# Attention and two MoE layers on one core: a second staging buffer for the weight chunks, gate constants pinned, fills sent later, and another split of the first dense unit's roundings

## The chip, the cores and the metric

One core of one Trainium2 chip runs the whole program in one launch. The metric is the device time of that launch in microseconds (us). Engines by the names of the profile: PE is TensorE, DVE is VectorE, ACT is ScalarE, POOL is GpSimd, SP is SyncE, which issues most DMAs.

## What is computed

The reference chains three parts, the output of one being the input of the next:

```
def phi(x):
    proj = np.einsum('bhsd,df->bhsf', x, w_phi)
    proj = proj - np.max(np.abs(proj), axis=-1, keepdims=True)
    return np.concatenate([np.exp(proj), np.exp(-proj)], axis=-1)
q_p, k_p = (phi(q), phi(k))
kv = np.einsum('bhsf,bhsd->bhfd', k_p, v)
z = np.sum(k_p, axis=2)
num = np.einsum('bhsf,bhfd->bhsd', q_p, kv)
den = np.einsum('bhsf,bhf->bhs', q_p, z)[..., None] + 1e-06
attn = num / den                      # 8 batches, 8 heads, 576 x 64
...
h = x @ w_in                          # 4608 x 512 @ 512 x 2048
g = h * np.cos(h)
x = g @ w_out                         # dense layer
...
logits = x @ w_gate + modality_bias[modality_id]
e_idx = np.argmax(logits, axis=1)     # top 1 of 8 experts
h = np.maximum(x[mask] @ w1[e], 0.0)
out[mask] = gate_w[mask, None] * (h @ w2[e])
```

`w_in` and `w_out` of the dense layer arrive as float64, two 32-bit words a number; the kernel has to make float32 parts of them itself.

## The kernel before

**Attention (L47 to L278).** The 64 (batch, head) pairs are taken in 16 items of two batches and two heads. An item has five turns; a turn handles up to two chunks of 128 tokens of both heads. In a turn PE transposes q and k (L121), ACT copies them out of PSUM (L124), PE projects them (L136), DVE takes the maximum of the absolute values (L141; the `m_q` reduction is a turn's first DVE instruction) and subtracts it (L142), ACT makes the exponentials of k (L153, L154), PE transposes the q side (L189), ACT makes the exponentials of q (L195, tiles `qx`, 5 buffers), PE sums the products of k and v (L174) and, for the item before, the quotient's parts (L210); DVE divides (L215 to L217), PE turns the result (L226), ACT copies it (L228) and an item's result leaves by one DMA (L231). The order of these is written out as a generator; each `next(att)` is one half turn, ten of them an item. Instructions inside `keep(...)` stay in program order on their engine; the others are placed by the tile framework's scheduler, within what buffers allow.

**Decode of the dense weights (L387 to L442).** The two dense weights are cut into 32 chunks of 512 KB, in the order of `seq`. `stage()` sends the DMA of the next chunk (L395 for `w_in`, L397 for `w_out`) into a staging tile `st`; `decoding()` makes two float32 parts of it: ACT takes abs of the high words (L431, or L418 in the form without steps), DVE does four passes of 128x512 (L432 to L435, or L419 to L423) of which the last two read the chunk again, ACT rounds to the high part (L436 or L424), `stage()` is called for the next chunk, and POOL makes the low part (L428; DVE L427 in the paced form). Fourteen chunks are decoded in steps during items 1 to 11 of attention (`work`, four calls an item), all pinned; the call that ends one chunk also makes the abs and the first pass of the next, so three calls make a chunk; six more, not pinned, during the last 20 half turns (`head`); twelve more, the paced ones, are decoded in three parts a round inside the first dense unit. For the first 14 chunks the staging tile is the one buffer `sx`; later chunks go to `raw_k` and `raw_q`. So a chunk's DMA is sent when the chunk before it has been read for the last time.

**Dense layer.** Nine units of 512 tokens, each with 16 slices of 128 columns. A round is 12 matmuls of 128x512 into `ph` (L472) for one slice, 12 matmuls into four accumulators (L506) for the slice three back, and `act()` (L481 to L498): ACT rounds ph/(2 pi) to integers `n` (L485), DVE subtracts (L487), ACT sine and square (L489, L490), DVE `g` (L492), DVE rounds `g` to its high part `gh` (L494), POOL takes the rest `gl` (L495). `split_x` makes the two parts of the next unit's x: DVE rounds (L462), POOL or, for the fourth, DVE subtracts (L463).

**Constants.** `consts()` (L973) writes four fills to DRAM, `tab` (L978) and rows of `x1d` (L981, L984), then runs `gate_consts` (L281), which loads the gate's weight and the modality ids (`mi`, L292, L293) and prepares small tiles on DVE. It is started at half turn 9 of attention and goes on at 17 to 25.

The rest (the gate, the routing, the experts) the change doesn't touch.

```
for n in range(170-TAIL):
    next(att)
    if n==8: stage()
    if n==9: next(setup)
    ...
    if 10<=n and n%10 in (0,2,4,6): next(work,None)
```

Of the kernel before, what the change touches and what calls it, by code (L numbers as in the profile page):

```python
# [11 lines left out]
F32 = mybir.dt.float32  # L12
# [18 lines left out]

SHARED = {"raw_k":(1024,2),"raw_q":(1024,2),"ke":(1024,4),"qe":(1024,3),"xT":(1152,4),"xw":(1024,6),"kt":(512,3),"qt":(512,3),"kvh":(512,4),"kvl":(512,4),"kvt":(512,2),"wx":(1024,5),"sx":(1024,1)}

def shared_tiles(tc, ctx):
    sp=ctx.enter_context(tc.tile_pool(name="shared",bufs=1))
# [6 lines left out]
def attention(tc, ctx, S, ps, ident, q, k, v, w_phi, xt):  # L44
# [138 lines left out]
    def qexp(i,g):  # L183

        n=GR[g][1]; tt=ts.pop(("q",i,g))
        pt=ps.tile([P,512],F32,tag="tr",name=f"ptt_{i}_{g}")
        for c in range(n):
            for s in range(2):
                keep(nc.tensor.transpose(pt[:,(2*c+s)*P:(2*c+s+1)*P],tt[:,(s*n+c)*F:(s*n+c+1)*F],ident))  # L189
        w=n*P  # L190
        x=qx[i,g]=ap.tile([P,1024],F32,tag="qx",name=f"qx_{i}_{g}",bufs=5)[:,:4*w].rearrange("p (h k c) -> p h k c",h=2,k=2)
        def vec():
            pv=pt[:,:2*w].rearrange("p (h c) -> p h c",h=2)
            for kk,sign in ((0,1.0),(1,-1.0)):
                nc.scalar.activation(x[:,:,kk,:],pv,AF.Exp,scale=sign)  # L195
        return vec
# [86 lines left out]
def gate_consts(tc, ctx, cpool, ps, ident, modality_id, modality_bias, w_gate, wgt, tp):  # L283
# [35 lines left out]
    nc.sync.dma_start(wgt[:,:],gt)  # L319
    yield  # L320

    nc.vector.memset(f32(g2[:,:,8:16]),0.0)
    fold=cpool.tile([16,8],F32,name="fold")
    V("tensor_tensor",fold,ident[0:16,0:8],ident[0:16,8:16],ALU.add)
    tri=cpool.tile([P,P],BF16,name="tri"); V("tensor_copy",tri,tf)
    one=cpool.tile([P,P],BF16,name="one"); nc.vector.memset(one,1.0)
    rev=cpool.tile([P,8],F32,name="rev"); V("tensor_copy",rev,ri)
    run=cpool.tile([P,8],F32,name="run0"); V("tensor_copy",run,rg)
    base=cpool.tile([P,8],F32,name="base"); V("tensor_copy",base,rg)
# [1 line left out]

    num=cpool.tile([P,8],F32,name="num"); V("tensor_copy",num,nm)
    slot=cpool.tile([1,25],F32,name="slot"); V("tensor_copy",slot,sl)
    ones=cpool.tile([1,16],F32,name="ones"); nc.vector.memset(ones,1.0)
    mf=tp.tile([P,36],F32,name="mf"); V("tensor_copy",mf,mi[:,:,:,0].rearrange("p a c -> p (a c)"))
    mz=tp.tile([P,36],F32,name="mz"); V("tensor_scalar",mz,mf,-1.0,1.0,op0=ALU.mult,op1=ALU.add)
    yield
# [8 lines left out]
def moes(tc, ctx, consts, S, ps, ident, att, end_att, xt, w_in, w_out, x1d, tab, wgt, w1, w2, out):  # L346
# [13 lines left out]
        return S({"fr":"kt","n":"qt","gh":"kvh","gl":"kvl"}[tag],name,dt)  # L360
    def pair(tag,name):

        if tag=="wl": t=late[0].tile([P,1024],F32R,tag="wl",name=name,bufs=12)
        else: t=S(tag,name,F32R)
        return t[:,0:512],t[:,512:1024]
    pj=[]
# [36 lines left out]
    def decoding(paced=False,steps=False):  # L403

        x=next(todo,None)
        if x is None: return
        decoded[0]+=1
        f,which=x
        v=st[f,which].rearrange("p (f w) -> p f w",w=2)
        H=v[:,:,1]; L=v[:,:,0]  # L410
        t=xtile("gl" if decoded[0]<=19 else "row",f"d_t{which}_{f}",F32)
        ti=t.bitcast(I32)
        h,l=pair(wtag[which][f],f"w{which}_{f}")
        (win,wout)[which][f]=(h,l)
        keep=tc.keep_in_program_order if paced else lambda ins: ins
        def one():

            nc.scalar.activation(t,H.bitcast(F32),AF.Abs,scale=2.0**-112)  # L418
            keep(nc.vector.tensor_scalar(t,t,F32_MAX,None,op0=ALU.min))  # L419
            keep(nc.vector.tensor_scalar(ti,ti,3,None,op0=ALU.logical_shift_left))  # L420
        def two():
            keep(nc.vector.scalar_tensor_tensor(ti,L,29,ti,op0=ALU.logical_shift_right,op1=ALU.bitwise_or))
            keep(nc.vector.scalar_tensor_tensor(ti,H,-0x80000000,ti,op0=ALU.bitwise_and,op1=ALU.bitwise_or))  # L423
            nc.scalar.copy(h,t)  # L424
            stage()
        def three():
            if paced: keep(nc.vector.tensor_tensor(l,t,f32(h),ALU.subtract))  # L427
            else: nc.gpsimd.tensor_tensor(l,t,f32(h),ALU.subtract)  # L428
        if steps:
            keep=tc.keep_in_program_order  # L430
            keep(nc.scalar.activation(t,H.bitcast(F32),AF.Abs,scale=2.0**-112))  # L431
            yield keep(nc.vector.tensor_scalar(t,t,F32_MAX,None,op0=ALU.min))  # L432
            yield keep(nc.vector.tensor_scalar(ti,ti,3,None,op0=ALU.logical_shift_left))
            yield keep(nc.vector.scalar_tensor_tensor(ti,L,29,ti,op0=ALU.logical_shift_right,op1=ALU.bitwise_or))
            keep(nc.vector.scalar_tensor_tensor(ti,H,-0x80000000,ti,op0=ALU.bitwise_and,op1=ALU.bitwise_or))  # L435
            keep(nc.scalar.copy(h,t)); stage(); three()  # L436
        elif paced: parts.append([one,two,three])
        else:
            one(); two(); three()
# [41 lines left out]
    def act(u,f):  # L481

        ph=phs.pop((u,f))
        n=xtile("n",f"n_{u}_{f}",I32)
        nc.scalar.activation(n,ph,AF.Copy,scale=INV2PI)  # L485
        g=xtile("fr",f"fr_{u}_{f}",F32)
        nc.vector.scalar_tensor_tensor(g,ph,INV2PI,n,op0=ALU.mult,op1=ALU.subtract)  # L487
        decode_part(2); decode_part(0)
        nc.scalar.activation(g,g,AF.Sin,scale=math.pi)  # L489
        nc.scalar.activation(g,g,AF.Square)  # L490
        score(1)
        nc.vector.scalar_tensor_tensor(g,g,-0.5,ph,op0=ALU.add,op1=ALU.mult)  # L492
# [451 lines left out]
def kernel(  # L944
# [27 lines left out]

    def consts():  # L973
        with tc.tile_pool(name="fill", bufs=1) as tp:
            pre = tp.tile([P, 8 * REG // P, 2], I32, name="pre")
            nc.gpsimd.memset(pre[:, :, 0], NTOK)
            nc.gpsimd.memset(pre[:, :, 1], 0)
# [48 lines left out]
```

## Time and profile before

| | before |
|---|---|
| median of 3 runs | 1726.19 us (1724.95 to 1727.88) |
| profiled execution, its own time | 1725.87 us |
| span of the profiled execution | 1723.9 us |
| PE busy | 1635.5 us (95%) |
| DVE busy | 1148.1 us (67%) |
| ACT busy | 828.2 us (48%) |
| POOL busy | 428.6 us (25%) |
| granted PE clock, mean | 0.976 of full speed |

How to read it: busy time is the sum of an engine's instructions, the span is from the first to the last of them. In the rows further down, `A <- B` behind a line says what that instruction waited for last, and the number ahead of it how long the engine stood idle. PEclk is the clock granted to PE as a share of full speed. A row of a window has its start and end and its length in us, then the busy us of PE, of PE's weight loads, DVE, ACT and POOL (each with the count of instructions), PEclk, the busy share of the DMA engines, and GB/s.

### The profile page before, as it was taken

What the parts mean: (1) busy time and instruction counts of PE and PEld (TensorE: products, weight loads), DVE (VectorE), ACT (ScalarE), POOL (GpSimd) and SP (SyncE); (2) the same over time, 40 slices, a digit from 0 to 9 for tenths busy, and PEclk for the clock granted to TensorE, in tenths of its full rate; (3) what the DMA queues carried; (4) which work ended last, traced back from release to release, by engine and by line L of the source; (5) the groups of instructions that cost most, each with busy time, mean ns of one, the idle gap of its engine ahead of it and who ended that gap; (6) DMA issues with size and microseconds to landing.
All of it is one profiled execution on the core that took longest, in us unless ns stands there. A gap on an engine that the chain in (4) does not pass through costs nothing.

```text
span 1723.9 us, 33528 instructions
## 1 busy us (share of the span) xinstructions
PE 1635.5 (95%) x13076; PEld 1397.7 (81%) x13076; DVE 1148.1 (67%) x2331; ACT 828.2 (48%) x1529; POOL 428.6 (25%) x353
## 2 busy tenths in 40 slices
PE   7898889989989999999999999999799999999997
PEld 5788878988768888888888888888678998899986
DVE  4677768786866767777776767664556655655635
ACT  4556657665433333334343434343335655655645
POOL 0000000003232333333333333342221221111212
PEclk8899989999989999999999999999899999999999
DMA  6434444433221010101010101000368675766656
GB/s 192 116 117 136 116 121 136 141 110 100 75 75 36 7 44 7 38 13 38 13 38 13 38 13 37 7 2 24 122 199 316 223 241 195 253 220 217 224 177 223
DMA packets 142544, 190.06 MB, mean 110 GB/s; under 512 B 64535, under 2 KB 89239, under 8 KB 142370
## 3 DMA queue, kind: packets, MB, share of 16 engines
q1 hardware_dynamic: 134578, 166.74, 30.7%
q0 software_dynamic: 7792, 21.02, 3.7%
q8 instruction: 108, 1.77, 0.4%
q14 instruction: 66, 0.54, 0.1%
HBM read 157.98 MB, written 30.51 MB: 109 GB/s over the span
## 4 chain that ended last, share of the span: by engine, by line
PE 72%; DVE 12%; DMA 8%; ACT 3%; issue 3%; SPq 1%; POOL 1%; DVEq 0%; POOLq 0%; ACTq 0%
PE ph L472 19%; PE acc L506 14%; PE mh L756 11%; PE po L768 10%; PE acc L511 4%; PE pj L136 3%; DMA st<-in_moe_w_in_dram 3%; PE pn L210 3%; PE kv L174 2%; DMA tab<-rec,pi 1%; DMA st<-in_moe_w_out_dram 1%; DVE x L462 1%; PE pt L121 1%; DMA raw<-in_moe_w_dram 1%; DVE d_t L423 1%
## 5 line engine op out<-in xcount | busy, mean ns | idle before, releaser
L472 PE MATMUL ph<-x,w 128*128 128x512 f32 x1728 | 425.7, 394 | 10.9 <-DVE x L462 5.9
L472 PEld LDWEIGHTS ph<-x,w 128*128 128x128 f32 x1728 | 322.8, 188 | 87.7 <-DVE x L462 9.6
L495 POOL TENSOR_TENSOR gl<-fr,gh 128x512 fp32r<-128x512 f32 x144 | 216.9, 1509 | 443.6 <-DVE gh L494 390.2
L716 DVE TENSOR_TENSOR m<-raw,m 128x512 fp32r<-128x512 f32 x320 | 210.2, 695 | 142.3 <-ACT m L715 142.3
L506 PE MATMUL acc<-w,gh 128*128 128x512 f32 x896 | 276.8, 390 | 0.0
L715 ACT CAST m<-raw 128x512 fp32r<-128x512 f32 x320 | 187.2, 618 | 69.3 <-PE mh L756 33.4
L756 PEld LDWEIGHTS mh<-xT,m 128*128 128x128 f32 x1728 | 212.3, 194 | 7.1 <-DVE hl L759 2.2
L756 PE MATMUL mh<-xT,m 128*128 128x256 f32 x1728 | 213.4, 285 | 4.6 <-DVE hl L759 2.0
L485 ACT ACTIVATE n<-ph 128x512 int32<-128x512 f32 x144 | 85.8, 596 | 269.1 <-PE ph L472 268.9
L506 PEld LDWEIGHTS acc<-w,gh 128*128 128x128 f32 x896 | 169.0, 189 | 35.1
L487 DVE SCALAR_TENSOR_TENSOR fr<-ph,n 128x512 f32<-128x512 f32 x144 | 99.2, 689 | 133.2 <-ACT n L485 117.7
L768 PE MATMUL po<-m,hh 128*128 128x512 f32 x576 | 181.3, 396 | 2.0 <-ACT hh L758 2.0
L536 DVE SCALAR_TENSOR_TENSOR junk<-x1T,wg 128x512 f32<-128x512 f32 x224 | 180.9, 808 | 0.0
L506 PE MATMUL acc<-w,gl 128*128 128x512 f32 x448 | 174.8, 390 | 0.0
L489 ACT ACTIVATE fr<-fr 128x512 f32<-128x512 f32 x144 | 91.1, 633 | 153.6 <-DVE fr L487 153.0
L492 DVE SCALAR_TENSOR_TENSOR fr<-fr,ph 128x512 f32<-128x512 f32 x144 | 98.7, 685 | 77.2 <-ACT fr L490 77.2
L768 PEld LDWEIGHTS po<-m,hh 128*128 128x128 f32 x576 | 106.0, 190 | 22.4 <-ACT hh L758 2.4
L806 POOL DMA_INDIRECT out_dram<-o,mrec x39 | 41.6, 1068 | 289.6 <-ACT o L805 281.0
L768 PE MATMUL po<-m,hl 128*128 128x512 f32 x288 | 113.1, 393 | 0.1
L210 PE MATMUL pn<-kvz,qx 128*64 128x65 f32 x2304 | 90.2, 233 | 18.7 <-DVE xs L217 16.5
L210 PEld LDWEIGHTS pn<-kvz,qx 128*64 128x64 f32 x2304 | 79.5, 145 | 29.5 <-issue 16.5
L506 PEld LDWEIGHTS acc<-w,gl 128*128 128x128 f32 x448 | 84.4, 188 | 17.7
(197 smaller groups left out, 2366.9 us busy)
## 6 DMA issues: line engine op xcount, KB each, us to landing
raw<-in_moe_w_dram SPq DMA_DIRECT2D x171, 512.0 KB
xt<-xo SPq DMA_DIRECT2D x16, 576.0 KB
xr<-xt SPq DMA_DIRECT2D x36, 256.0 KB
raw_k<-in_k_dram SPq DMA_DIRECT2D x32, 256.0 KB
raw_q<-in_q_dram SPq DMA_DIRECT2D x32, 256.0 KB
v<-in_v_dram SPq DMA_DIRECT2D x64, 128.0 KB
st<-in_moe_w_in_dram SPq DMA_DIRECT2D x16, 512.0 KB
st<-in_moe_w_out_dram SPq DMA_DIRECT2D x16, 512.0 KB
```

Source lines behind the costliest of these rows:

```text
L210: keep(nc.tensor.matmul(o[64*c:64*c+64],x[:,h,sg,t*P+64*c:t*P+64*c+64],kvs[i,bb][:,2*h+sg,:],start=sg==0,stop=sg==1,skip_group_check=True))
L472: nc.tensor.matmul(ph,A[:,ws],xhl[u,d][k],start=n[0]==0,stop=n[0]==11); n[0]+=1
L487: nc.vector.scalar_tensor_tensor(g,ph,INV2PI,n,op0=ALU.mult,op1=ALU.subtract)
L489: nc.scalar.activation(g,g,AF.Sin,scale=math.pi)
L492: nc.vector.scalar_tensor_tensor(g,g,-0.5,ph,op0=ALU.add,op1=ALU.mult)
L495: nc.gpsimd.tensor_tensor(gl,g,f32(gh),ALU.subtract)
L506: nc.tensor.matmul(accs[u][c],A[:,ws],B,start=(f==0 and k==0),stop=(f==NF-1 and k==2))
L536: return lambda: tc.keep_in_program_order(nc.vector.scalar_tensor_tensor(junk,x1T[u,c],1.0,wg[e],op0=ALU.mult,op1=ALU.mult,accum_out=lgs[u ...
L715: keep(nc.scalar.copy(h,a))
L716: keep(nc.vector.tensor_tensor(l,a,f32(h),ALU.subtract))
L756: nc.tensor.matmul(ph[:,f2*T:(f2+1)*T],A[:,ws],B[d//2][:,xs],start=n==0,stop=n==11); n+=1
L768: nc.tensor.matmul(po[c],A[:,ws],B,start=(f==0 and j==0),stop=(f==NF2-1 and j==2))
```

## The change

It gives `sx` two buffers and the tile of the q exponentials four in place of five. The first chunk is staged at half turn 4 and the second at 14, where before the first was staged at 8 and the others each at the end of the decode ahead of it; with the calls of `stage()` inside the decode left as they are, a chunk is from then on staged one decode earlier. The table of staging tiles follows (16 chunks in `sx`, then `raw_k`, `raw_q`), one more chunk is decoded ahead of the first dense unit (21, with a new place in `head`), and the pool `wl` has 11 buffers for 12. The three memsets of the gate constants are pinned. The four fills are written behind the gate constants, at half turn 25. In `act()`, in the rounds that carry a paced decode, ACT makes `gh` and DVE makes `gl`.

```
-...,"sx":(1024,1)}
+...,"sx":(1024,2)}
...
-        x=qx[i,g]=ap.tile([P,1024],F32,tag="qx",name=f"qx_{i}_{g}",bufs=5)[...]
+        x=qx[i,g]=ap.tile([P,1024],F32,tag="qx",name=f"qx_{i}_{g}",bufs=4)[...]
...
-    nc.vector.memset(f32(g2[:,:,8:16]),0.0)
+    V("memset",f32(g2[:,:,8:16]),0.0)
...
-        return S(turn(("sx",)*14+("raw_k",)*5 if n<19 else ("raw_k","raw_k","raw_q"),"stg"),name,I32)
+        return S(turn(("sx",)*16+("raw_k",)*3 if n<19 else ("raw_k","raw_k","raw_q") if n<24 else ("raw_k",),"stg"),name,I32)
...
-    early=["wx"]*5+["qe"]*3+["xw"]*6+["xT"]*4+["raw_q","sx"]
+    early=["wx"]*5+["qe"]*3+["xw"]*6+["xT"]*4+["raw_q","sx","sx"]
...
-        nc.vector.tensor_copy(gh,g)
-        nc.gpsimd.tensor_tensor(gl,g,f32(gh),ALU.subtract)
+        if parts:
+            nc.scalar.copy(gh,g)
+            nc.vector.tensor_tensor(gl,g,f32(gh),ALU.subtract)
+        else:
+            nc.vector.tensor_copy(gh,g)
+            nc.gpsimd.tensor_tensor(gl,g,f32(gh),ALU.subtract)
...
-        if n==8: stage()
+        if n in (4,14): stage()
...
-    for n in (1,5,10,12,15,17): head.setdefault(n,[]).append(lambda: decoded[0]<len(early) and decode())
+    for n in (1,5,10,12,15,17,18): head.setdefault(n,[]).append(lambda: decoded[0]<len(early) and decode())
...
         with tc.tile_pool(name="fill", bufs=1) as tp:
+            yield from gate_consts(tc, ctx, cpool, ps, ident, modality_id, modality_bias, w_gate, wgt, tp)
             pre = tp.tile([P, 8 * REG // P, 2], I32, name="pre")
...
-            yield from gate_consts(tc, ctx, cpool, ps, ident, modality_id, modality_bias, w_gate, wgt, tp)
```

How it moves instructions, at three places. First SP's queue behind the loads of the third item (`st` is a staged chunk, `tab` and `x1d` the fills, `wgr`, `mi`, `mb` the gate's inputs, `raw_k` and `rl_k` an item's k). Before:

```order
L67 DMA rl_q_190<-in_q_dram 64x2x64
L395 DMA st_0_355<-in_moe_w_in_dram 128x4x256
L978 DMA tab<-pre 128x608
L981 DMA x1d<-zero 1x512
L984 DMA x1d<-zero 128x512 x4
L288 DMA wgr<-in_moe_w_gate_dram 128x4x8
L292 DMA mi<-in_moe_modality_id_dram 128x4x8
```

And now, with the place to which the fills went:

```order
L67 DMA rl_q_190<-in_q_dram 64x2x64
L395 DMA st_0_239<-in_moe_w_in_dram 128x4x256
L288 DMA wgr<-in_moe_w_gate_dram 128x4x8
L292 DMA mi<-in_moe_modality_id_dram 128x4x8
...
L66 DMA raw_q_519<-in_q_dram 128x2x256 x2
L395 DMA st_0_613<-in_moe_w_in_dram 128x4x256
L983 DMA tab<-pre 128x608
L986 DMA x1d<-zero 1x512
L989 DMA x1d<-zero 128x512 x2
L66 DMA raw_k_949<-in_k_dram 128x2x256 x2
```

The fills moved behind the gate's inputs, the next item's loads and the second chunk.

Second, DVE where item 1's first turn begins (`m_q` is a turn's first reduction, `mf` the cast of the modality ids, `t_q` the q side). Before:

```order
L286 CAST mf<-mi 128x36
L286 TENSOR_SCALAR mz<-mf 128x36
L141 TENSOR_REDUCE m_q_0_497<-pj_0_452 128x4
L432 TENSOR_SCALAR d_t_0_448<-d_t_0_448 128x512
L142 TENSOR_TENSOR t_q_0_457<-pj_0_452,m_q_0_497 128x512
L141 TENSOR_REDUCE m_k_0_500<-pj_0_452 128x4
```

And now the same turn, and further on the second turn of item 2, which has the cast:

```order
L141 TENSOR_REDUCE m_q_0_486<-pj_0_441 128x4
L432 TENSOR_SCALAR d_t_0_437<-d_t_0_437 128x512
L142 TENSOR_TENSOR t_q_0_446<-pj_0_441,m_q_0_486 128x512
...
L286 CAST num<-nm 128x8
L286 CAST slot<-sl 1x25
L286 MEMSET ones 1x16
L286 CAST mf<-mi 128x36
L286 TENSOR_SCALAR mz<-mf 128x36
L434 SCALAR_TENSOR_TENSOR d_t_1_686<-st_0_613,d_t_1_686 128x512
L141 TENSOR_REDUCE m_q_1_1007<-pj_1_962 128x4
L142 TENSOR_TENSOR t_q_1_967<-pj_1_962,m_q_1_1007 128x512
```

The cast and what is made of it moved five turns and more further back. On ACT, not shown here, the abs of the first chunk that isn't pinned now stands directly behind the abs of the last pinned one, ahead of a turn's copies out of PSUM, where before it stood further on.

Third, DVE in one round of the first dense unit (`fr` is g, `d_t` a chunk in decode, `w` its low part). Before, and behind it now:

```order
L487 SCALAR_TENSOR_TENSOR fr_5_6822<-ph_5_6793,n_5_6820 128x512
L427 TENSOR_TENSOR w_12_6772<-d_t_12_6771,w_12_6772 128x512
L419 TENSOR_SCALAR d_t_9_6818<-d_t_9_6818 128x512
L420 TENSOR_SCALAR d_t_9_6818<-d_t_9_6818 128x512
L492 SCALAR_TENSOR_TENSOR fr_5_6822<-fr_5_6822,ph_5_6793 128x512
L494 CAST gh_5_6831<-fr_5_6822 128x512
L422 SCALAR_TENSOR_TENSOR d_t_9_6818<-st_1_6744,d_t_9_6818 128x512
L423 SCALAR_TENSOR_TENSOR d_t_9_6818<-st_1_6744,d_t_9_6818 128x512
```

```order
L487 SCALAR_TENSOR_TENSOR fr_5_6835<-ph_5_6806,n_5_6833 128x512
L423 SCALAR_TENSOR_TENSOR d_t_9_6784<-st_1_6656,d_t_9_6784 128x512
L427 TENSOR_TENSOR w_9_6785<-d_t_9_6784,w_9_6785 128x512
L419 TENSOR_SCALAR d_t_13_6831<-d_t_13_6831 128x512
L492 SCALAR_TENSOR_TENSOR fr_5_6835<-fr_5_6835,ph_5_6806 128x512
L420 TENSOR_SCALAR d_t_13_6831<-d_t_13_6831 128x512
L496 TENSOR_TENSOR gl_5_6845<-fr_5_6835,gh_5_6844 128x512
L422 SCALAR_TENSOR_TENSOR d_t_13_6831<-st_0_6670,d_t_13_6831 128x512
```

The cast L494 is gone, the subtraction L496 has come from POOL, and the last pass over a chunk (L423) has moved behind the next round's L487.

## Rows read from the trace of the kernel before

**Rows 1.** The page: PE's busy time, and the chain that ended last.
```profile
PE 1635.5 (95%) x13076; PEld 1397.7 (81%) x13076; DVE 1148.1 (67%) x2331; ACT 828.2 (48%) x1529; POOL 428.6 (25%) x353
...
PE 72%; DVE 12%; DMA 8%; ACT 3%; issue 3%; SPq 1%; POOL 1%; DVEq 0%; POOLq 0%; ACTq 0%
```
**Rows 2.** Busy time by window: items 0, 1, 2, 10, 12, then five turns.
```profile
7.87:36.51 28.64, 21.98 (x282) 16.89 (x281) 12.82 (x24) 15.71 (x33) 0.00 (x0) 0.92 0.72 193
36.51:67.76 31.25, 24.28 (x338) 22.09 (x340) 19.53 (x49) 11.89 (x28) 1.40 (x2) 0.69 0.42 114
67.76:94.61 26.85, 23.57 (x409) 21.44 (x411) 18.59 (x47) 15.01 (x34) 1.40 (x2) 0.87 0.38 109
...
263.72:286.02 22.30, 20.62 (x407) 18.72 (x409) 17.75 (x44) 16.00 (x38) 2.68 (x3) 1.00 0.53 155
...
307.49:327.99 20.50, 20.41 (x407) 18.59 (x409) 15.59 (x37) 13.51 (x33) 0.13 (x1) 1.00 0.41 118
...
255.33:276.10 20.77, 20.48 (x408) 18.59 (x410) 17.65 (x42) 14.00 (x33) 1.41 (x2) 1.00 0.44 135
```
**Rows 3.** Waits of ACT, 40 to 400 us: total us, times, longest us.
```profile
ACT d_t L431 <- DMA st<-in_moe_w_in_dram: 29.9, 8, 5.6
ACT d_t L431 <- DMA st<-in_moe_w_out_dram: 8.6, 5, 2.7
```
**Rows 4.** The same view for SP's queue.
```profile
SPq L66 <- PE pt L121: 78.8, 10, 13.4
```
**Rows 5.** The timeline of one such wait: start us, us, what, [idle before <-releaser].
```profile
98.56 0.37 SPq L395 DMA_DIRECT2D st<-in_moe_w_in_dram  x1
...
104.17 0.66 ACT L431 ACTIVATE d_t<-st 128x512 f32<-128x512 f32 x1 [3.58 <-DMA st<-in_moe_w_in_dram]
...
105.76 0.69 PE L210 MATMUL pn<-kvz,qx 128*64 128x65 f32 x16 [3.13 <-DVE xs L217]
```
**Rows 6.** The timeline where item 1 begins: first chunk, ids, projection.
```profile
31.69 0.68 ACT L431 ACTIVATE d_t<-st 128x512 f32<-128x512 f32 x1 [1.37 <-DMA st<-in_moe_w_in_dram]
...
36.19 0.18 DVE L286 CAST mf<-mi 128x36 f32<-128x36 int32 x1 [7.79 <-DMA mi<-in_moe_modality_id_dram]
...
39.59 1.23 PE L136 MATMUL pj<-w,qT 64*128 64x128 f32 x8 [6.93 <-DVE rd L216]
```
**Rows 7.** Busy time by window: eight rounds of dense unit 0, its end.
```profile
438.57:490.10 51.53, 45.54 (x193) 35.31 (x191) 42.57 (x65) 24.46 (x41) 12.31 (x8) 1.00 0.28 87
490.10:500.50 10.40, 5.90 (x13) 3.45 (x13) 9.33 (x11) 1.88 (x3) 6.83 (x5) 0.64 0.20 76
```
**Rows 8.** The chain, in order of time: one round without decode.
```profile
504.69 2.72 PE ph L472 x12
507.41 2.72 PE acc L506 x12
```
**Rows 9.** Groups by form, 420 to 490 us: busy us, mean ns | idle.
```profile
L423 DVE SCALAR_TENSOR_TENSOR d_t<-st,d_t 128x512 int32<-128x512 int32 x11 | 17.4, 1578 | 0.3
...
L424 ACT CAST w<-d_t 128x512 fp32r<-128x512 f32 x11 | 6.8, 620 | 21.7 <-DVE d_t L423 21.7
L494 DVE CAST gh<-fr 128x512 fp32r<-128x512 f32 x11 | 4.7, 426 | 0.9
```
**Rows 10.** The timeline: an L423 alone, then a round of dense unit 0.
```profile
412.74 0.68 DVE L423 SCALAR_TENSOR_TENSOR d_t<-st,d_t 128x512 int32<-128x512 int32 x1
...
463.67 3.01 PE L472 MATMUL ph<-x,w 128*128 128x512 f32 x12 [1.08 <-DVE fr L492]
...
464.31 1.58 POOL L495 TENSOR_TENSOR gl<-fr,gh 128x512 fp32r<-128x512 f32 x1 [5.25 <-DVE gh L494]
464.78 1.67 DVE L423 SCALAR_TENSOR_TENSOR d_t<-st,d_t 128x512 int32<-128x512 int32 x1
```
**Rows 11.** The timeline of the end of dense unit 0.
```profile
491.98 1.48 DVE L462 CAST x<-xr 128x512 fp32r<-128x512 f32 x1
...
493.52 1.22 PE L472 MATMUL ph<-x,w 128*128 128x512 f32 x2 [2.68 <-DVE x L462]
```

More of the change, by code (lines that the diff above doesn't have):

```diff
@@ L30, in f32 @@
     return ap.bitcast(F32)
-SHARED = {"raw_k":(1024,2),"raw_q":(1024,2),"ke":(1024,4),"qe":(1024,3),"xT":(1152,4),"xw":(1024,6),"kt":(512,3),"qt":(512,3),"kvh":(512,4),"kvl":(512,4),"kvt":(512,2),"wx":(1024,5),"sx":(1024,1)}
+SHARED = {"raw_k":(1024,2),"raw_q":(1024,2),"ke":(1024,4),"qe":(1024,3),"xT":(1152,4),"xw":(1024,6),"kt":(512,3),"qt":(512,3),"kvh":(512,4),"kvl":(512,4),"kvt":(512,2),"wx":(1024,5),"sx":(1024,2)}
 def shared_tiles(tc, ctx):
@@ L190, in qexp @@
         w=n*P
-        x=qx[i,g]=ap.tile([P,1024],F32,tag="qx",name=f"qx_{i}_{g}",bufs=5)[:,:4*w].rearrange("p (h k c) -> p h k c",h=2,k=2)
+        x=qx[i,g]=ap.tile([P,1024],F32,tag="qx",name=f"qx_{i}_{g}",bufs=4)[:,:4*w].rearrange("p (h k c) -> p h k c",h=2,k=2)
         def vec():
@@ L325, in gate_consts @@
     tri=cpool.tile([P,P],BF16,name="tri"); V("tensor_copy",tri,tf)
-    one=cpool.tile([P,P],BF16,name="one"); nc.vector.memset(one,1.0)
+    one=cpool.tile([P,P],BF16,name="one"); V("memset",one,1.0)
     rev=cpool.tile([P,8],F32,name="rev"); V("tensor_copy",rev,ri)
@@ L333, in gate_consts @@
     slot=cpool.tile([1,25],F32,name="slot"); V("tensor_copy",slot,sl)
-    ones=cpool.tile([1,16],F32,name="ones"); nc.vector.memset(ones,1.0)
+    ones=cpool.tile([1,16],F32,name="ones"); V("memset",ones,1.0)
     mf=tp.tile([P,36],F32,name="mf"); V("tensor_copy",mf,mi[:,:,:,0].rearrange("p a c -> p (a c)"))
@@ L361, in pair @@
     def pair(tag,name):
-        if tag=="wl": t=late[0].tile([P,1024],F32R,tag="wl",name=name,bufs=12)
+        if tag=="wl": t=late[0].tile([P,1024],F32R,tag="wl",name=name,bufs=11)
         else: t=S(tag,name,F32R)
@@ L410, in decoding @@
         H=v[:,:,1]; L=v[:,:,0]
-        t=xtile("gl" if decoded[0]<=19 else "row",f"d_t{which}_{f}",F32)
+        t=xtile("gl" if decoded[0]<=20 else "row",f"d_t{which}_{f}",F32)
         ti=t.bitcast(I32)
@@ L692, in alloc_w @@
             tag=wtag[1][n]
-            t=late[0].tile([P,1024],F32,tag="wl",name=f"raw_{n}",bufs=12) if tag=="wl" else S(tag,f"raw_{n}",F32)
+            t=late[0].tile([P,1024],F32,tag="wl",name=f"raw_{n}",bufs=11) if tag=="wl" else S(tag,f"raw_{n}",F32)
             RAW.append(t[:,0:1024])
```

## The prediction

> **What bounds the kernel now.** I read the page first: PE is busy for 95% of the span and is 72% of the chain that ended last, DVE 12% and DMA 8% [rows 1]. So a gain can only come from stretches in which PE waits or runs at a lower clock. Next the windows by item of attention, to find them [rows 2]. The item at 307.49 holds no stepped decode and takes 20.50 us with PE busy for 20.41. Five turns from 255.33 hold one whole stepped decode whose chunk was in place, and take 20.77. That is the bound which decode leaves: 0.27 a chunk. Item 0 takes 28.64, item 1 31.25, items 2 to 10 together 286.02 - 67.76 = 218.26, a mean of 24.25. Against 20.8 an item these lose 7.8, 10.5 and 31. Third, the waits, to see who is late: ACT's abs of a chunk waits 29.9 + 8.6 us, 13 times, for the DMA of its chunk [rows 3]. One of them shows the way of the delay [rows 5]: the DMA is sent at 98.56, the abs begins at 104.17, after 3.58 us of idle ACT; what stands behind it on ACT is late, and PE's L210 begins at 105.76, having been idle for 3.13. Items 0 and 1 have another cause: SP sends the fills first, the modality ids come behind them, and DVE, in order, stands 7.79 us at the ids' first cast; PE's next projection begins after 6.93 us of idling [rows 6].
>
> Then the dense part. A round without decode is 2.72 + 2.72 = 5.44 us, all PE [rows 8]. Eight rounds with decode take 51.53, or 6.44 each, with DVE busy for 42.57 of it, and the unit's end takes 10.40 where the next matmul group alone would need 2.72 [rows 7].
>
> **The change part by part.**
>
> *Staging an item ahead.* A chunk's DMA needs 104.17 - 98.56 = 5.6 us from issue to use [rows 5]; a decode takes three of an item's four calls, some 15 us, and with two buffers one whole decode now lies between. The abs' wait goes for chunks 2 to 13. Cover: these 15 us. It is gone if SP sends late; the loads ahead of a chunk on SP's queue wait up to 13.4 us [rows 4], but a chunk's place among them is the same as its forerunner's was, so I count the stall at zero, with a bound below. Items 2 to 10 go from 218.26 to 9 x 20.8 = 187.2, which is -31.1. Within this lies the lower clock: item 2 was granted 0.87 of full speed, item 12 1.00 [rows 2], and PE's busy time was 23.57 against 20.41, so half of that item's loss is clock after idling, which goes with the idling. What is late next: the first unpinned chunk. Its abs stands right behind that of the last pinned one on ACT, ahead of a turn's copies, while its own buffer has come free only with the chunk two before. I charge it one half of a stall of [rows 5], and as much for the next: +2 in all. The bounds for items 2 to 10: nothing left, -31; a third of the waits left because SP's queue is late, -20.
>
> *Fills and gate constants.* By the change's order the cast of the ids has moved from ahead of item 1's first turn to item 2's second, so DVE's wait of 7.79 [rows 6] goes in full, whenever the fills go. Item 0 falls by nearly all of PE's 6.93 us: -6.7, to 21.9 (its other excess, the first loads, stays). Item 1 would fall to 20.8, with two additions. The pinned gate constants, memsets included, put some sixteen small operations of about 0.18 us [rows 6] into DVE's turns, several of which before ran ahead of the first turn: 2.9 us of DVE in all, of which I put 1.5 on the path, as DVE has 3 us of room in an item [rows 2]. And the first chunk stands behind the same loads on SP as before, so its abs still comes at about 31.69, after ACT's 1.37 of waiting [rows 6]; with DVE no longer held until 36.19, its pass over that chunk, pinned behind the turn's first reduction, now waits for it: +2. So item 1 comes to 24.3 (-7.0). The five fills go later, their sends at some 0.4 us each [rows 5] or 2 in all, in front of the next item's k; that load is an item ahead, which hides it; without the cover it is +2 once. Bounds for both items: -16.8 (no cost) and -9. `qx` at 4 buffers: its reuse waits for reads that PE, in order, has made before; nothing.
>
> Items 11 to 15 I leave as they are: a few chunks there are still sent just ahead of their abs. Attention: -31.1 + 2 - 6.7 - 7.0 = -42.8.
>
> *The entry to the dense unit.* One more chunk is decoded ahead of it, unpinned. On DVE its first pass stands ahead of the fourth subtraction of x, on which the first L1 waits. If its DMA is as late as that of [rows 5], half its stall of 3.58 falls on PE: +2. From below zero; from above a whole 5.6.
>
> *The first dense unit.* Why 6.44 and not 5.44? DVE's last pass L423 takes 1578 ns on average in the unit [rows 9] where it takes 0.68 alone [rows 10]; in the round shown it runs from 464.78 while POOL's L495 runs from 464.31 to 465.89, and ends 0.56 behind it: about 0.9 lost, on the path to the next round, as PE waits 1.08 for DVE [rows 10]. The Trainium skill (SBUF — State Buffer, Who interferes with whom) says that a DVE instruction with two SBUF inputs contends with a GpSimd instruction that reads SBUF, over a port pair that is an exclusive lock; the trace agrees, 1.67 beside L495 against 0.68 alone. Now POOL makes no `gl` in these rounds. DVE's share: minus L494 0.426, plus L496 at 0.68 (the two-input pass alone [rows 10]), minus 0.9 of blocking: -0.6 a round. DVE's own sum is then 0.69 x 6 (L487, L422, L423, L427, L492, L496) + 2 x 0.42 = 5.0, to which come waits for ACT's two roundings. The rounding costs 0.620 on ACT against 0.426 on DVE, and ACT is busy for only 24.46 of 51.53 [rows 7, 9], so it has room, but DVE must wait for it: 0.3 to 0.6 a round. 5.3 to 5.6 against PE's 5.44: I take 5.5, so 8 rounds give -7.5, and bounds are -8.0 and -2 (DVE at 6.2, every handoff in series).
>
> A rule against this edit: the Trainium skill (Perfetto Trace Analysis, Optimizing Scalar/DVE Operations) says that DVE is the faster where it has a performance mode, and that moving work to Scalar may pay if DVE is saturated. The rows bear out the first half, 0.426 against 0.620, and nearly the condition of the second, DVE being busy for 83% of the eight rounds [rows 7]; by the first half alone the rounds would keep their 6.44 and the sum would end at 1682.
>
> *The unit's end.* The 10.40 hold casts of x at 1.48 beside POOL [rows 11] (0.426 for L494, a cast of that size [rows 9]), and a PE wait of 2.68; the clock falls to 0.64 [rows 7]. The loads on POOL stay, since L463 is untouched, but `gl` and a paced decode leave: of 10.40 - 2.72 = 7.7 I give back 5, with 1 more of clock behind it. Bounds -7.7 and 0. Dense: -7.5 - 6 + 2 = -11.5, which less an allowance of 3 for rounds in which POOL's x parts meet the decode is -8.5.
>
> **Sum.** -42.8 - 8.5 = -51.3. The profiled execution took 1725.87 itself (span 1723.9, 2.0 outside it), 0.3 under the median, so the forecast is 1725.9 - 51.3, or **1675**.
>
> **The rivals.** *All of it goes.* The first chunks' leftovers and the end vanish too, -31 - 16.8 - 8 - 7.7 = -63.5, with some 5 more from items 13 to 15: about 1657. For it: PE's busy time leaves room. Against: two abs side by side on ACT. Chance 0.12.
>
> *DVE takes PE's place.* In the five turns without a stall DVE is busy for 17.65 of 20.77 [rows 2]; pinned decode and pinned gate operations leave it little slack, so any lateness is kept in every item, and the dense rounds stay at 6.2. Attention then recovers two thirds, -30, dense -6: 1690. The rule above would give its dense half. For it: DVE is 12% of the chain; against: these same five turns ran at PE's speed. Chance 0.20.
>
> *Slower: SP sends late anyway.* The chunk stands on SP behind k loads that wait for PE's reads, 78.8 us in 10 waits [rows 4]. From the point at which these hold a chunk back by more than about 10 us (15 less the 5.6 it needs) the second buffer gives nothing. As every abs is pinned, the stalls then stay, and the fills, now ahead of a load of k, hold up an item by as much as they do before; the 1.5 of gate operations and 2 at the dense entry are added: +3.5, 1729. For it: the longest wait is 13.4. Against: a mean of 7.9. Chance 0.02.
>
> *It doesn't do what it says.* The scheduler puts unpinned decode ahead and DMA and abs stay adjacent; ACT's order shows this for one chunk, so only the ids' wait and the dense unit gain: -13.7 - 8.5, 1704. Chance 0.04.
>
> **How the numbers follow.** My forecast has 0.62, the five cases sum to 1. Its own bounds are 1664 to 1685. For 8 in 10 the range takes in the first two rivals, 1657 to 1692. A measurement of this kernel tells 0.2%, 3.5 us, from no change. Faster by more than that: every case but the slower one, 0.98, of which 0.02 goes to same, for a gain smaller than any here: 0.96, 0.02 and 0.02.
>
> **What would show it.** Items 2 to 10 at 20.8 each (the first a little more), with PEclk 1.00, and no ACT wait for `st` over 0.5 us before the fourteenth chunk; DVE's wait for the ids gone and item 0 near 22; L423 at 0.7 in the dense unit and its rounds at 5.5; an end of 5. Wrong it would be if DVE is what PE waits for in every turn, if the waits for `st` are still near 38 us, or if the fills' DMA on SP holds up an item's loads.

## The result and the profile after

The changed kernel takes 1684.99 us (median of 4 runs, 1683.05 to 1687.10) where the kernel before took 1727.04 beside it (4 runs, 1724.95 to 1729.55): a ratio of 0.9756, 95% interval 0.9737 to 0.9776. That is 42 us less. The forecast was 1675, 51 less, with a range from 1657 to 1692. The profiled execution of the changed kernel took 1687.10 us itself (span 1685.2), 2 above its median. The page still has PE busy nearly throughout, and DMA has lost 3 points of the chain, DVE has gained 2 (compare [rows 1]):

```profile
PE 1623.7 (96%) x13076; PEld 1387.0 (82%) x13076; DVE 1143.0 (68%) x2330; ACT 835.9 (50%) x1540; POOL 412.3 (24%) x343
...
PE 70%; DVE 14%; DMA 5%; ACT 5%; issue 4%; SPq 1%; POOL 1%; another core or an unknown queue 0%; POOLq 0%; DVEq 0%; ACTq 0%
```

The windows tell where the time went. First items 0 and 1 together, items 2 to 10, items 11 to 14, the rounds from the fourth to the seventeenth L1 of the first dense unit (13 of them), and that unit's end; columns as in [rows 2]. Before:

```profile
7.87:67.76 59.89, 46.26 (x620) 38.98 (x621) 32.35 (x71) 27.60 (x61) 1.40 (x2) 0.80 0.56 152
67.76:286.02 218.26, 192.78 (x3647) 175.14 (x3649) 160.86 (x386) 133.98 (x305) 16.27 (x21) 0.95 0.45 129
286.02:374.20 88.18, 82.92 (x1619) 75.39 (x1620) 72.90 (x171) 58.27 (x134) 5.57 (x8) 0.98 0.47 137
410.73:490.10 79.37, 73.38 (x320) 58.30 (x316) 64.33 (x104) 38.15 (x67) 19.70 (x13) 1.00 0.36 111
490.10:504.52 14.42, 9.92 (x24) 6.64 (x25) 10.96 (x14) 3.74 (x6) 7.25 (x5) 0.64 0.15 55
```

And the same five stretches of the changed kernel:

```profile
9.61:54.55 44.94, 41.31 (x620) 33.72 (x621) 32.20 (x76) 27.60 (x61) 1.41 (x2) 1.00 0.74 202
54.55:260.87 206.32, 189.07 (x3648) 171.72 (x3650) 170.85 (x395) 136.61 (x307) 16.57 (x21) 0.98 0.49 140
260.87:346.49 85.62, 81.31 (x1619) 73.90 (x1621) 68.31 (x163) 56.26 (x128) 4.31 (x7) 1.00 0.41 122
383.85:456.56 72.71, 72.35 (x319) 58.09 (x316) 59.99 (x106) 45.19 (x80) 6.64 (x5) 1.00 0.41 131
456.56:465.97 9.41, 7.83 (x25) 5.33 (x25) 7.65 (x10) 3.12 (x5) 5.53 (x4) 0.82 0.02 7
```

The differences are -15.0, -11.9, -2.6, -6.7 and -5.0, together -41.1. Only the second is far from its term in the forecast, -31.1 with 2 given back: the stretch for which the second buffer was made gained a good third of what was expected. (The two profiled spans differ by 38.7: in the changed kernel item 0 begins 1.7 us later, and the entry and the first three rounds take 0.8 more. Item 0 begins at 7.9 to 9.9 over the kernels here.)

Yet the wait that the buffer was to remove has gone altogether. Among ACT's waits for a chunk between 30 and 372 us not one is left for a stepped chunk (L431; 29.9 + 8.6 us in [rows 3]); these two rows are for chunks that aren't pinned:

```profile
ACT d_t L418 <- DMA st<-in_moe_w_out_dram: 3.4, 2, 2.8
ACT d_t L418 <- DMA st<-in_moe_w_in_dram: 2.8, 1, 2.8
```

PE, however, in items 2 to 10 still waits ten times for DVE's reciprocal (total us, times, longest):

```profile
PE pj L136 <- DVE rd L216: 15.1, 10, 2.0
```

What holds DVE there is shown by the chain of work that ended last, followed through one such turn of the changed kernel (start us, us, what):

```profile
81.00 0.52 ACT ke L154
81.51 0.51 ACT w L436
82.02 0.59 ACT d_t L431
82.61 0.02 issue
82.63 1.02 DVE d_t L432
83.65 0.60 DVE m_k L141
84.25 0.07 DVE rd L215
84.32 0.66 DVE t_k L142
84.98 0.10 DVE rd L216
85.07 0.05 issue
85.12 1.09 PE pj L136 x8
```

The call that ends a chunk's decode also begins the next. With the chunk in place, its abs (L431) runs at once behind the rounding cast of the chunk before (L436), and DVE's first pass L432, pinned between two reductions of the turn, first waits for the abs and then takes 1.02 us. The groups of the two kernels by line, items 2 to 10, show that this length is new. Before:

```profile
L431 ACT ACTIVATE d_t<-st 128x512 f32<-128x512 f32 x12 | 8.0, 664 | 34.5 <-DMA st<-in_moe_w_in_dram 25.9 <-DMA st<-in_moe_w_out_dram 8.6
L432 DVE TENSOR_SCALAR d_t<-d_t 128x512 f32<-128x512 f32 x12 | 5.1, 427 | 25.1 <-ACT d_t L431 25.1
```

After:

```profile
L428 POOL TENSOR_TENSOR w<-d_t,w 128x512 fp32r<-128x512 f32 x12 | 15.3, 1275 | 131.2 <-ACT w L436 131.2
L432 DVE TENSOR_SCALAR d_t<-d_t 128x512 f32<-128x512 f32 x12 | 12.4, 1033 | 6.7 <-ACT d_t L431 6.7
```

1033 ns in place of 427. The same cast L436 that the abs stands behind also sends POOL's low part L428 on its way, which lasts 1.28 us and now meets L432. Before, the DMA's lateness kept the two apart; this is the shortest wait of all, in the five turns of [rows 2]:

```profile
265.40 1.28 POOL L428 TENSOR_TENSOR w<-d_t,w 128x512 fp32r<-128x512 f32 x1 [22.16 <-ACT w L436]
...
266.57 0.67 ACT L431 ACTIVATE d_t<-st 128x512 f32<-128x512 f32 x1 [1.25 <-DMA st<-in_moe_w_out_dram]
...
267.27 0.43 DVE L432 TENSOR_SCALAR d_t<-d_t 128x512 f32<-128x512 f32 x1 [0.74 <-ACT d_t L431]
```

So nine of the twelve chunk ends still cost PE 1.3 to 1.8 us of waiting; the tenth wait, 1.95 us at 259.67, is that of the first chunk that isn't pinned. In items 3, 6 and 9 the granted clock falls as well, to a mean of 0.93 (0.98 over the stretch). The other three ends, in items 2, 5 and 8, cost PE next to nothing, though L432 takes 1.03 us there too: in item 5 it starts at 133.69, when DVE's reciprocal of that turn has run at 132.48, and items 5 and 8 take 20.5 us each. What costs is thus a late and long L432 that stands ahead of the reciprocal.

### The profile page after: what moved, and what is told of

Same layout as the page of the kernel before. It is cut to its first block, busy times and chain, and to the rows that moved or that the text cites. A ratio compares the mean times of both kernels' runs of the same rounds, so it can differ in the third digit from the quotient of the medians.

```text
span 1685.2 us, 33568 instructions
## 1 busy us (share of the span) xinstructions
PE 1623.7 (96%) x13076; PEld 1387.0 (82%) x13076; DVE 1143.0 (68%) x2330; ACT 835.9 (50%) x1540; POOL 412.3 (24%) x343
## 4 chain that ended last, share of the span: by engine, by line
PE 70%; DVE 14%; DMA 5%; ACT 5%; issue 4%; SPq 1%; POOL 1%; another core or an unknown queue 0%; POOLq 0%; DVEq 0%; ACTq 0%
PE ph L472 19%; PE acc L510 14%; PE mh L760 11%; PE po L772 11%; PE acc L515 4%; PE pj L136 3%; PE pn L210 2%; PE kv L174 2%; DMA tab<-rec,pi 2%; DVE x L462 2%; DVE t_k L142 1%; DMA raw<-in_moe_w_dram 1%; PE pt L121 1%; DVE m_k L141 1%; DVE m_q L141 1%
## 5 line engine op out<-in xcount | busy, mean ns | idle before, releaser
L499 POOL TENSOR_TENSOR gl<-fr,gh 128x512 fp32r<-128x512 f32 x133 | 199.7, 1503 | 388.6 <-DVE gh L498 323.7
L487 DVE SCALAR_TENSOR_TENSOR fr<-ph,n 128x512 f32<-128x512 f32 x144 | 99.2, 689 | 137.3 <-ACT n L485 119.9
L489 ACT ACTIVATE fr<-fr 128x512 f32<-128x512 f32 x144 | 91.1, 632 | 162.2 <-DVE fr L487 161.5
L490 ACT ACTIVATE fr<-fr 128x512 f32<-128x512 f32 x144 | 90.9, 631 | 4.0
L141 DVE TENSOR_REDUCE m_q<-pj 128x4 f32<-128x512 f32 (+1 forms) x80 | 50.9, 637 | 59.5 <-PE pj L136 58.7
```

## The experiments

Twelve kernels in three groups. Each was compared with the kernel before on its own chip, and the chips differ: the median of the kernel before was 1725.65, 1729.42 and 1722.61 us in the three groups. So the ratios are told beside the times, and the stage windows of the profiles decide.

**What is left in items 2 to 10: one call more per chunk.** The edit, in the changed kernel and, alone, in the kernel before:

```
-            keep(nc.scalar.copy(h,t)); stage(); three()
+            keep(nc.scalar.copy(h,t)); stage(); yield three()
```

> One call more per stepped chunk: the abs of the next chunk no longer follows the last pass of this one in the same call, but four half turns later; 14 chunks by 4 calls just fill items 1 to 14. Theory (the rest of the loss in items 2 to 10 is a pile-up: abs stands behind the rounding cast on ScalarE for 0.8 us, and the first VectorE pass, beside GpSimd's low part, takes 1.02 in place of 0.43, so TensorE idles 1.3 to 1.8 us a chunk and its clock dips thereafter): L432 at 0.43, no wait for the abs, items 2 to 10 together at 188 to 192 against 206.3, whole kernel 1666 to 1672. Rival (VectorE is full, 18 of 20.8 us an item, and any place of the passes costs the same): items 2 to 10 stay above 202, kernel 1681 to 1688.

> The kernel before with that same additional call and nothing else: one staging buffer, but the abs now comes four half turns (some 8.4 us) after the DMA was sent, which needs 5.6. Theory (what costs is that abs and DMA are adjacent, not that there is one buffer): the 38 us of ScalarE waits for chunks in items 1 to 11 fall under 6, items 2 to 10 from 218 to 188 to 193, kernel 1697 to 1703. Rival (a second buffer is needed, since SyncE sends late): waits stay above 20 us, kernel 1715 to 1727.

Measured: 1670.92 us, ratio 0.9680 (0.9628 to 0.9732), and 1688.84, ratio 0.9782 (0.9727 to 0.9837). Items 2 to 10 of the first, and then of the second:

```profile
53.42:241.66 188.24, 183.82 (x3648) 167.28 (x3650) 156.54 (x378) 130.39 (x299) 12.64 (x18) 1.00 0.50 145
```

```profile
60.58:248.75 188.17, 183.81 (x3647) 167.30 (x3649) 156.16 (x374) 130.22 (x299) 12.63 (x18) 1.00 0.49 141
```

Both have the 188 that the theory gave, at a clock of 1.00. In the changed kernel with the gap, one chunk's end and the next chunk's start look like this in the timeline, two turns apart:

```profile
75.64 0.69 ACT L431 ACTIVATE d_t<-st 128x512 f32<-128x512 f32 x1
76.37 0.43 DVE L432 TENSOR_SCALAR d_t<-d_t 128x512 f32<-128x512 f32 x1 [0.30 <-ACT d_t L431]
...
87.53 0.64 ACT L436 CAST w<-d_t 128x512 fp32r<-128x512 f32 x1
87.63 0.54 SPq L397 DMA_DIRECT2D st<-in_moe_w_out_dram  x1
88.25 1.27 POOL L428 TENSOR_TENSOR w<-d_t,w 128x512 fp32r<-128x512 f32 x1 [6.55 <-ACT w L436]
...
96.52 0.69 ACT L431 ACTIVATE d_t<-st 128x512 f32<-128x512 f32 x1
97.24 0.43 DVE L432 TENSOR_SCALAR d_t<-d_t 128x512 f32<-128x512 f32 x1 [0.30 <-ACT d_t L431]
```

L432 is back at 0.43. The DMA is sent at 87.63 and the abs comes 8.9 us later, time enough even for the single buffer, where DMA and abs are of the same chunk: the kernel before with this `yield` gains 30 us in items 2 to 10, its waits for stepped chunks are gone as well, and as a whole (1688.84) it was faster than was expected of it (1697 to 1703). Items 0 and 1 gained too, 50.95 against 59.89, which I hadn't counted. The rival that a second buffer is needed falls. That DVE is full isn't decided by these two: with one more call a chunk, items 2 to 10 hold nine stepped chunks in place of twelve, and each ends at the same place in its item. The first chunk that isn't pinned moves with them, from item 10 to item 14, and items 11 to 14 take 89.9 us with the gap where the changed kernel takes 85.6. The next run keeps number and place.

**The order of two neighbours on ACT.**

```
+            if decoded[0]<14:
+                y=seq[decoded[0]]
+                u=ahead[y]=xtile("gl",f"d_t{y[1]}_{y[0]}",F32)
+                keep(nc.scalar.activation(u,st[y]...,AF.Abs,scale=2.0**-112))
             keep(nc.scalar.copy(h,t)); stage(); three()
```

> The changed kernel with two neighbours on ScalarE exchanged: where a stepped decode ends, the abs of the next chunk stands ahead of the rounding cast of this one, everything else in its place (possible only with two staging buffers). Theory (the abs is late because it stands behind that cast, and with it VectorE's L432 slips onto GpSimd's L428): L432 starts 0.5 to 0.8 us sooner, ahead of L428, lasts 0.43, items 2 to 10 together 188 to 195 against 206.3, kernel 1667 to 1674. Rival (it is the crowding of that call, nine operations of decode in one half turn, and not the order of two of them): items 2 to 10 at 200 or more, kernel 1679 to 1686.

Measured: 1680.1 us, ratio 0.9720 (0.9699 to 0.9742). Items 2 to 10:

```profile
57.20:250.88 193.68, 184.56 (x3647) 167.32 (x3649) 163.40 (x393) 135.19 (x307) 16.77 (x21) 1.00 0.51 148
```

```profile
L432 DVE TENSOR_SCALAR d_t<-d_t 128x512 f32<-128x512 f32 x12 | 5.1, 427 | 3.5 <-ACT d_t L439 3.4
```

The stretch is 193.7, inside the theory's 188 to 195, and L432 took 427 ns in all twelve. In items 2 to 9, which hold no unpinned chunk in any of the three, the changed kernel takes 180.8 us, this one 169.3 and the one with the gap 167.4: 11.5 of the 13.4 us that the gap gives there come from putting one ACT instruction ahead of another, with the same chunks at the same places. So the rival of crowding falls for this stretch, and with it the one that DVE is full. The whole kernel was slower than the 1667 to 1674 expected and lies in the rival's range; items 0 and 1 took 2.9 more than in the changed kernel, and what follows the first dense unit, which the edit doesn't touch, 5.0 more (1224.3 against 1219.2; in the other kernels it is 1214.9 to 1221.3). For neither was a cause looked for.

**Five calls an item.** `n%2==0` in place of `n%10 in (0,2,4,6)`, with the gap.

> The changed kernel with the additional call per chunk and five calls an item in place of four, so that the 14 chunks end in item 11 or 12 as in the changed kernel and the first chunks that aren't pinned don't crowd item 14. Theory: items 2 to 10 at 188 to 193 as with four calls, since a gap of one turn behind the last pass is enough, items 11 to 14 at 86 against 89.9, kernel 1664 to 1670. Rival (at a steadily moving place in the item the passes meet the short turns, and part of the pile-up comes back): items 2 to 10 at 197 or more, kernel 1673 to 1680.

Measured: 1674.82 us, ratio 0.9703 (0.9683 to 0.9722), items 2 to 10 at 191.2, now with 11 to 12 chunks in them, items 11 to 14 at 89.9. The first is as expected; the second isn't, and the time is in the rival's range: the unpinned chunks cost as much in items 11 and 13 as with four calls in item 14. It is no better than the plain gap.

**The gate constants.** The pinned memsets alone, and the fills' move alone, in the kernel before.

> The kernel before with the three memsets of the gate constants pinned, nothing else. Theory (it is the pinning that moves the cast of the ids to the second turn of item 2, so the fills' place in the queue doesn't matter): VectorE's wait for the ids is gone, item 0 at 22 against 28.6; item 1 keeps its wait for the second chunk, so items 0 and 1 together 50 to 54 against 59.9, kernel 1716 to 1721. Rival (the fills' DMAs themselves take the time): items 0 and 1 at 58 or more, kernel 1724 to 1728.

> The kernel before with the fills behind the gate constants, memsets not pinned, nothing else. In VectorE's order the cast of the ids then still stands ahead of item 1's first turn. Theory: the ids come some 4 us sooner, so VectorE's wait falls from 7.8 to 3 to 5 us and not to zero; items 0 and 1 together 55 to 58, kernel 1720 to 1725. Rival (the fills were the whole cause): wait under 1 us, items 0 and 1 at 52 or less, kernel 1715 to 1719.

Measured: 1724.6 us, ratio 0.9977 (0.9957 to 0.9997), and 1727.82, ratio 1.0000 (0.9982 to 1.0017); items 0 and 1 together 56.5, between the first theory and its rival, and 57.4, as the second theory has it. Both kernels lie above the range of their theory. The waits explain the stretch. With the fills later and nothing pinned, DVE waits for the ids as long as before (first 68 us of the launch):

```profile
DVE mf L286 <- DMA mi<-in_moe_modality_id_dram: 7.7, 1, 7.7
```

So the theory's 3 to 5 us was wrong, and the rival's under 1 too: the ids come sooner, but the cast comes as much sooner in DVE's order. With the memsets pinned the wait is gone, and item 0 takes 21.8; but ACT now waits for the second chunk, which with one buffer is sent late, and item 1 takes 34.8:

```profile
ACT d_t L431 <- DMA st<-in_moe_w_in_dram: 9.1, 2, 8.3
```

Items 2 to 10 of this kernel took 223.0, 4.8 more than before; no cause was looked for.

**The staging undone, all else as changed.** One buffer, chunks staged as before.

> The changed kernel with one staging buffer, chunks staged as before, 20 chunks ahead of the dense unit. Theory (the second buffer takes the DMA wait away, but the pile-up behind it takes its place, so that only about 12 us of the 31 lost in items 2 to 10 come back): items 2 to 10 at 215 to 220, kernel 1696 to 1701. Rival (the prediction's step, the second buffer is worth 31 us): kernel 1712 to 1718.

Measured: 1716.21 us, ratio 0.9938 (0.9913 to 0.9964). The time is the rival's, its reason isn't. Items 0 and 1, and items 2 to 10:

```profile
8.48:64.87 56.39, 43.15 (x619) 36.40 (x622) 31.82 (x76) 27.92 (x61) 1.40 (x2) 0.85 0.61 160
64.87:284.54 219.67, 195.11 (x3647) 177.51 (x3649) 161.51 (x389) 134.24 (x305) 16.30 (x21) 0.95 0.44 128
```

Items 2 to 10 lose 13.3 against the changed kernel, as the theory has it; items 0 and 1 lose 11.5, again by the second chunk, and the first unit's end 3.1. Some 3.5 of the 15 us of items 0 and 1 come without that chunk in time (56.4 here and 56.5 with the memsets pinned alone, for 59.9); the rest comes only where it is there.

**The first dense unit.** gh and gl back as they were; then each of the two alone.

> The changed kernel with the rounding of g on VectorE and the rest on GpSimd in all rounds, as before. Theory (GpSimd's gl blocks VectorE's L423 and, at the unit's end, the casts of x): rounds of the first unit back to 6.4, its end from 9.4 back to about 14, kernel 1694 to 1698. Rival (the end shrank because one chunk fewer is left to the unit): only the rounds come back, kernel 1690 to 1692.

> The changed kernel with gl on GpSimd again while gh stays on ScalarE: VectorE is relieved of the rounding, but GpSimd runs beside it. Theory (what made the rounds 6.3 is GpSimd's subtraction blocking VectorE's two-input passes, not the 0.43 of the rounding): a two-input pass still takes 1.5 or more in each round, rounds 3 to 16 of the first unit 77 to 83 us together against 72.7, kernel 1690 to 1696. Rival (VectorE's load decided it): rounds 3 to 16 at 71 to 74, kernel 1684 to 1687.

> The changed kernel with gh on VectorE again while gl stays there too: GpSimd is out, VectorE has 0.43 more a round but no longer waits for ScalarE's rounding (0.35 in the rounds of the changed kernel). Theory: rounds 3 to 16 at 72 to 75 us, kernel 1684 to 1688, so ScalarE's part of the edit is worth next to nothing. Rival (VectorE is at its limit at 5.5 a round): rounds 3 to 16 at 77 to 79, kernel 1689 to 1692.

Measured: 1697.02 us, ratio 0.9829 (0.9776 to 0.9883); 1682.72, ratio 0.9755 (0.9716 to 0.9795); 1684.06, ratio 0.9751 (0.9705 to 0.9797). The same 13 rounds, in this order:

```profile
381.89:464.44 82.55, 74.12 (x320) 58.05 (x316) 68.56 (x107) 39.21 (x69) 23.50 (x16) 1.00 0.37 116
```

```profile
380.88:453.05 72.17, 71.76 (x320) 58.87 (x317) 57.00 (x96) 45.89 (x80) 23.25 (x16) 1.00 0.43 133
```

```profile
384.91:457.68 72.77, 72.44 (x320) 58.47 (x317) 63.30 (x118) 38.13 (x69) 6.11 (x5) 1.00 0.41 130
```

Undone, the rounds lose 9.8 us, 3.2 more than they took in the kernel before, and L423 takes 1668 ns again. But either half of the edit alone gives all of it: with gl on GpSimd (busy for 23.25 us) the rounds are as short as without, against my theory, and so they are with both on VectorE, as expected. What came with the move is seen in the groups of eight rounds with gl on GpSimd, and in one of these rounds:

```profile
L496 POOL TENSOR_TENSOR gl<-fr,gh 128x512 fp32r<-128x512 f32 x7 | 11.0, 1571 | 27.4 <-ACT gh L495 27.4
L423 DVE SCALAR_TENSOR_TENSOR d_t<-st,d_t 128x512 int32<-128x512 int32 x9 | 7.2, 800 | 0.3
```

```profile
409.79 0.69 DVE L423 SCALAR_TENSOR_TENSOR d_t<-st,d_t 128x512 int32<-128x512 int32 x1
409.89 1.75 POOL L496 TENSOR_TENSOR gl<-fr,gh 128x512 fp32r<-128x512 f32 x1 [3.51 <-ACT gh L495]
```

gl waits for ACT's rounding and so starts behind L423, where in the kernel before it started 0.47 us ahead of it [rows 10]. L423 then takes 0.69 us, and it is gl that is longer; from 403 us on L423 is ahead of gl in every round. What the theory had wrong is thus that POOL would still be first; that the rounds are long because POOL holds L423 up is borne out. They are short in the three kernels in which L423 takes some 0.7 us in all or nearly all of them, and long where it takes 1.6 to 1.7. DVE's load isn't the reason: its busy sum is 63.3 us with both on VectorE, in short rounds, and 68.6 undone, of which some 12 are the lengthening of twelve passes by 0.98 each. A single such meeting can still cost nothing: in the kernel before L423 took 1.66 us at 426.41 and at 433.09 while PE still began a round every 5.44 us; the rounds were longer from 438.57 on.

The unit's end stayed at 9.9 with the edit undone: the theory's 14 was wrong and its rival right, the end shrank because one paced chunk fewer runs into it. With the staging undone, where that chunk is back, it takes 12.5.

**Roundings of the second unit's x on ACT.** With the gap; `(nc.scalar.copy if u==1 else nc.vector.tensor_copy)(h,r)` in `split_x`.

> The kernel with one call more per stepped chunk (1670.9), and the four roundings of the second unit's x on ScalarE in place of VectorE. Theory (what is left of the first unit's end, 8.3 us against 5.4, is those roundings at 1.46 each beside GpSimd): the end at 5.6 to 6.8, kernel 1667 to 1670. Rival (the end waits for the x parts that GpSimd makes one after the other, 1.3 to 1.5 each, and for the order of VectorE): the end at 7.8 or more, kernel 1670 to 1673.

Measured: 1674.15 us, ratio 0.9709 (0.9669 to 0.9749); the end at 8.5 against 8.3. The time lies above both ranges; the end is the rival's case: in the timeline POOL takes a gl ahead of the third x part, and PE waits for that:

```profile
443.41 1.71 POOL L499 TENSOR_TENSOR gl<-fr,gh 128x512 fp32r<-128x512 f32 x1
...
445.09 1.44 POOL L463 TENSOR_TENSOR x<-xr,x 128x512 fp32r<-128x512 f32 x1
...
446.58 0.73 PE L472 MATMUL ph<-x,w 128*128 128x512 f32 x2 [2.58 <-POOL x L463]
```

**The gap without the second buffer.** The kernel with the staging undone, plus the gap.

> All of the change but the second staging buffer (one buffer, 20 chunks ahead), with one call more per stepped chunk. Theory (a turn between DMA and abs does what the buffer was to do): items 2 to 10 at 188 to 190, items 0 and 1 at 45 to 48, the first unit's end some 3 us longer for the additional paced chunk, kernel 1672 to 1679. Rival (the buffer is needed beside the gap): items 2 to 10 over 195, kernel 1682 or more.

Measured: 1670.61 us, ratio 0.9683 (0.9642 to 0.9725), items 0 and 1 at 45.1, items 2 to 10:

```profile
53.87:242.08 188.21, 183.84 (x3648) 167.29 (x3650) 156.62 (x378) 130.23 (x299) 12.62 (x18) 1.00 0.48 141
```

It is level with the gap on two buffers (0.9680), and both are below the changed kernel (0.9756, its interval beginning at 0.9737). Once DMA and abs are two turns apart, the second buffer gives nothing that these runs can tell.

## Why the prediction was right or wrong, point by point

*Direction, and the sum.* Faster, by 42 us for the 51 forecast. Four of the five terms were near: items 0 and 1 (-13.7 forecast, -15.0 measured), the rounds (-7.5, -6.7), the end (-6, -5.0, without the allowance of 3), items 11 to 14 (0, -2.6). The fifth, items 2 to 10, fell short by 17 us (-29.1 with the 2 given back, -11.9), outside the bounds of -31 and -20 that I gave. That the sum is off by 9 only is luck: the allowance of 3 for the rounds and most of the 2 at the entry weren't needed, and items 0 and 1 and items 11 to 14 gave 4 more than forecast.

*The step that failed: "Items 2 to 10 go from 218.26 to 9 x 20.8 = 187.2".* The abs' wait went, as the prediction says; the time that it had covered didn't, and the items measured 206.3, or 22.9 each. I priced a chunk in place at 0.27 us from five turns at 20.77 [rows 2]. That was misread: the chunk wasn't in place, its abs waited 1.25 us for its DMA (266.57, shown above), and every chunk before waited at least that long. So no row before showed an abs directly behind the cast, and the meeting that follows from it was in no term. The run with the two exchanged on ACT shows what took the wait's place: the abs behind L436, and L432 beside L428 at 1.03 us for 0.43. Without that meeting items 2 to 9 give back 11.5 us. The rival "DVE takes PE's place" had the symptom, PE waiting for DVE, but its cause, that DVE has no slack, is refuted: with the two exchanged DVE makes the same passes over the same chunks, and items 2 to 9 take 21.2 on average.

*"A chunk's place among the loads is the same as its forerunner's"*: held; no stepped chunk came late, and the slower rival had no case.

*The cast of the ids goes five turns back, "whenever the fills go"*: right as far as the wait; the pinning alone removes it and the fills' move alone doesn't. What I missed is that half of the time returns as a wait for the second chunk, so that pinning alone was worth 3.4 us in items 0 and 1. In the changed kernel, with its second buffer, the two edits pay together. The second buffer without the pinned constants wasn't run; nearest to it is the kernel before with the gap, in which the second chunk comes in time and the ids don't, at 50.95. The sends of the fills are six (1, 1 and 4), not the five that I counted; no term hung on it. The first chunk's wait, priced at 2, was 0.6 us of DVE's.

*The first chunk that isn't pinned* stalled as forecast, at 253.41, with 2.83 us of wait on ACT; item 10 takes 25.5 us where items 4 and 7, which like it hold two chunk ends, take 23.2. That is 2.3 more, near the 2 that I gave.

*The dense rounds*: the size was right, -7.1 over the eight rounds of [rows 7] for the -7.5 forecast, and so was the reason, POOL holding up L423. The split into DVE's share and ACT's wasn't needed: either half of the edit alone keeps L423 from being held up. The Trainium skill (Perfetto Trace Analysis, Optimizing Scalar/DVE Operations) has DVE as the faster where it has a performance mode. That did not decide: the rounding took 0.62 us on ACT and 0.42 on DVE, and the rounds were as long with it on either (72.7 and 72.8).

*The entry* was charged +2; the stretch from the last item's start to the first L1 stayed at 24.4 for 24.3, and the first three rounds took 13.0 for 12.2.

## What to carry to other kernels

Before pricing a wait at its full length, ask what it keeps apart: the operations that it separated can meet once it is gone, and what they then cost may stand in no row of the trace before. Where a transfer and its first use are adjacent in program order, moving the use by one step may do more than another buffer, and costs no memory. And where two edits each remove one of several waits of the same stretch, try them together too: here one alone handed half of the time to the other.

## What the runs showed that I had not expected

A DVE pass with a single input in SBUF (L432, 128x512, one constant) took 1033 ns beside a GpSimd subtraction and 427 alone, so not only the two-input passes are held up. The Trainium skill (SBUF — State Buffer, Who interferes with whom) says that tensor_scalar can enter a two-port mode, and that DVE contends with GpSimd in such a mode. The 1033 ns agree with it; whether L432 ran in that mode no row shows. In these rows it is the one that starts second that is held up. L432 started half a us behind L428, which took 1275 ns as before (1272). L423 took 1.67 us behind a gl that had started ahead of it, and 0.69 where it started 0.1 us ahead of gl, which then took 1.75 for the 1.29 that it takes where it meets nothing.
